# Another order of attention, polar work and weight decoding up to the third unit, and a later last sum of the weights' test

## The chip, the cores and the metric

The kernel runs on one core of a Trainium2 chip. The metric is the device time of one execution in microseconds; a time is the median of several runs. The engines are named as in the profile: PE multiplies matrices, DVE, ACT and POOL work on vectors, SP issues most of the transfers. "The profile" and "the trace" are those of one execution that the hardware profiler recorded.

## What is computed

Three stages follow one another. A linear attention with a complex decay for each channel, a feed-forward layer whose negative half is scaled by alpha, and a layer with eight experts, of which each token takes one:

```python
# attention: B, H, S, D = 4, 8, 768, 48
scale = np.minimum(mag, 0.999) / (mag + 1e-06)
for t in range(S):
    new_re = ar * S_re - ai * S_im
    new_im = ar * S_im + ai * S_re
    S_re, S_im = (new_re + k[t] v[t]^T, new_im)
    y[t] = q[t] @ S_re
# moe: 3072 tokens, 384 -> 2048 -> 384
h = x @ w_in
g = np.maximum(h, 0.0) + alpha * np.minimum(h, 0.0)
x = g @ w_out
# moe2: 8 experts, 384 -> 1024 -> 384
e_idx = np.argmax(x @ w_gate + modality_bias[modality_id], axis=1)
out[e_idx == e] = gate_w * (np.maximum(x @ w1[e], 0.0) @ w2[e])
```

The weights `w_in` and `w_out` of the second stage come as 64-bit floating point numbers.

## The kernel before

**Attention.** The sequence is cut into 6 chunks of 128 tokens, and with 4 batches that makes 24 steps k. For each step, or pair of steps, `polar_group` (L679 on) turns the decays into angles and lengths, runs three scans along the chunk (L737) and writes `z`, which holds the transformed q and k: four multiplications, L774 and L776 twice. `bounce` writes z to DRAM (`zd`) and `bounce_back` reads it turned (`qk`). `attn` then takes, in two halves of four heads, the scores `pa` (L807), the masked `at` (L809, on DVE), the transpose `pk` of k (L815) and its copy `ks`, the output `py` (L825), its split into `xt` and `t` (L831, L832), and the state's increment `pu` (L839, L843).

**The second stage.** A unit is 256 tokens, two steps. `moe1` runs each unit over 8 pairs p of two feature blocks. `l1` makes `ph` (L876, L877, L879; PSUM holds two of them), ACT and DVE make of it `n` (L884, L886), `gh` (L889) and, a turn later, `gl` (L864); `l2` adds to `acc` (L919) two turns later. A unit's first `ph` needs all of its `xt`.

**Decoding.** Each feature block's weights are 64-bit patterns which DVE turns into 32-bit numbers `wf` with three operations (L613, L616, L619), two blocks at a time. `weights_part` then takes a rounded copy on ACT (L566) and the rest on DVE (`w`, L567), and PE transposes the second half (`pl`, L571) so that the routing weights can be multiplied in (`og`, L585).

**The third stage** runs in units named s, t and f with `p2` (L486, L487, L490), `hh`, `hl` (L494), `a2` (L505); its weights `wr` are loaded and split into `wh` and `wl` (L475) as it goes. Beside it a test goes over the weights of the second stage (`ck`, `cm`, L967, L970), whose result `weights_flag` reduces to one number: on DVE (`fw_m`, L977), by a transpose on PE (`fw_t`, L980) and on DVE again (`fw_1`, L982; `fw_i`, L984). Its value enters `more`, which decides on a general fallback, and which SP loads into a register.

**What sets the order.** The program issues instructions to five in-order queues through a scheduler, so an engine takes its instructions in the order that the queue has, and waits where an operand is not there. Up to the third unit the order of issue is spelled out in two strings. START is done before `moe1`, TURN[g] at turn g of it. Each letter is one call: `x`, `y` one DVE operation of the polar work of steps 0 and 1, `q` of steps 2 and 3, `p` of steps 4 and 5; `A`, `a` a part of the attention of steps 0 and 1, `B` of steps 2 and 3, `C` of steps 4 and 5; `D` decodes a pair of weight blocks, `F` finishes one; `b`, `c` issue the bounces of z0 and z1, `d` the rest of the weight loads, `w` the warm-up of 28 products on z1; `<` and `>` switch on and off a link that keeps each step behind the last DVE instruction of the one before. `issue_after(i)` likewise puts what follows behind instruction i.

## Time and profile before

| | us |
|---|---|
| median of 3 runs | 913.98 |
| lowest and highest run | 911.38, 915.74 |
| the profiled execution | 912.0 |
| its span | 910.3 |
| busy: PE, DVE, ACT, POOL | 827.3, 676.0, 467.8, 209.3 |
| mean granted clock of PE | 0.957 of full |

The span is that of the instructions, the execution's own time has 1.7 us around it. "Busy" is the time in which an engine has an instruction running; PE's sum says nothing of the clock at which it runs, which the profile gives separately, as a part of full speed. In the timelines a bracket tells how long the engine was idle ahead of a row and which engine's result ended that.

### The profile page before, as it was taken

Reading aid. Unit: us, or ns where it says so; the run is one execution under the profiler, and the core shown is the slowest. Engines: PE = TensorE matmul, PEld = TensorE weight load, DVE = VectorE, ACT = ScalarE, POOL = GpSimd, SP = SyncE. Lnnn points to the kernel's source line nnn. Section 1 sums busy time; section 2 is a strip of 40 time slices with the busy share of each in tenths; the row PEclk is TensorE's granted clock in tenths of the full one; section 3 lists DMA queues with packets and bytes.
Section 4 is the critical chain, followed back from the end, with each engine's and each line's share of the span. In section 5 each row is a group of like instructions: output and inputs, shape, how many; then the busy total and the mean of one; then the engine's idle time right before and its main releaser. Section 6 shows DMA issues by size and latency. Waiting matters only on the chain.

```text
span 910.3 us, 16047 instructions
## 1 busy us (share of the span) xinstructions
PE 827.3 (91%) x5949; PEld 788.5 (87%) x5949; DVE 676.0 (74%) x1419; ACT 467.8 (51%) x871; POOL 209.3 (23%) x204
## 2 busy tenths in 40 slices
PE   0768978999979999999999999899999999999893
PEld 0658977989979999999999999899988888999893
DVE  7988797999978888878898989455644755666751
ACT  7634446856655655565656564232344445456450
POOL 2001311212102121211212121000332543534550
PEclk9858989999989999999999999999999999999997
DMA  8829400626455326262727261600355477677550
GB/s 330 249 99 317 138 1 4 205 98 176 135 137 154 66 102 152 89 166 67 189 66 189 67 188 32 144 23 6 123 168 143 152 231 258 202 232 268 162 181 20
DMA packets 63591, 130.37 MB, mean 143 GB/s; under 512 B 10456, under 2 KB 39656, under 8 KB 63504
## 3 DMA queue, kind: packets, MB, share of 16 engines
q1 hardware_dynamic: 59536, 119.49, 44.3%
q0 software_dynamic: 3968, 9.77, 3.3%
q8 instruction: 49, 0.80, 0.4%
q14 instruction: 38, 0.31, 0.1%
HBM read 98.17 MB, written 28.91 MB: 140 GB/s over the span
## 4 chain that ended last, share of the span: by engine, by line
PE 52%; DVE 15%; DMA 9%; issue 4%; ACT 1%; POOL 1%; SPq 0%; DVEq 0%; ACTq 0%; POOLq 0%
PE acc L919 12%; PE a2s L505 6%; PE ph L876 5%; PE ph L877 4%; PE ph L879 4%; DMA qk<-zd 4%; DMA zd<-z 3%; PE pa L807 3%; PE p2s L490 2%; DVE n L886 2%; PE p2s L486 2%; PE p2s L487 2%; PE pu L839 2%; PE py L825 1%; PE py L827 1%
## 5 line engine op out<-in xcount | busy, mean ns | idle before, releaser
L876 PE MATMUL ph<-xt,w 128*128 128x256 f32 x576 | 156.0, 299 | 9.6 <-DVE n L886 5.8
L919 PE MATMUL acc<-w,gh 128*128 128x392 f32 x768 | 161.1, 348 | 0.0
L877 PE MATMUL ph<-xt,w 128*128 128x256 f32 x576 | 149.9, 288 | 0.0
L919 PEld LDWEIGHTS acc<-w,gh 128*128 128x128 f32 x768 | 135.1, 192 | 0.6 <-issue 0.5
L876 PEld LDWEIGHTS ph<-xt,w 128*128 128x128 f32 x576 | 112.6, 196 | 11.6 <-DVE n L886 6.2
L886 DVE SCALAR_TENSOR_TENSOR n<-n,al,ph 128x256 f32<-128x256 f32 x192 | 84.1, 473 | 45.2 <-ACT n L884 44.9
L877 PEld LDWEIGHTS ph<-xt,w 128*128 128x128 f32 x576 | 112.9, 196 | 0.2 <-issue 0.2
L879 PE MATMUL ph<-xt,w 128*128 128x256 f32 x576 | 102.5, 287 | 2.1 <-DVE w L567 2.1
L884 ACT ACTIVATE n<-ph 128x512 f32<-128x512 f32 x96 | 57.0, 593 | 78.3 <-PE ph L879 77.3
L919 PE MATMUL acc<-w,gl 128*128 128x392 f32 x384 | 88.7, 345 | 0.0
L889 ACT CAST gh<-n 128x512 fp32r<-128x512 f32 x96 | 59.2, 617 | 57.2 <-DVE n L886 54.8
L864 DVE TENSOR_TENSOR gl<-n,gh 128x512 fp32r<-128x512 f32 x96 | 66.8, 696 | 27.8 <-ACT gh L889 27.7
L879 PEld LDWEIGHTS ph<-xt,w 128*128 128x128 f32 x576 | 84.1, 194 | 2.4 <-DVE w L567 2.3
L268 POOL DMA_INDIRECT tbl<-tok,ix x24 | 27.4, 1141 | 201.7 <-DVE ix L266 191.7
L807 PE MATMUL pa<-qk 96*128 96x128 f32 x384 | 57.0, 296 | 14.9 <-DMA qk<-zd 12.6
L919 PEld LDWEIGHTS acc<-w,gl 128*128 128x128 f32 x384 | 69.8, 190 | 0.4 <-issue 0.3
L807 PEld LDWEIGHTS pa<-qk 96*128 96x128 f32 x384 | 53.4, 207 | 18.0 <-issue 7.7
L494 DVE SCALAR_TENSOR_TENSOR hls<-p2s,hhs 128x512 fp32r<-128x512 f32 x32 | 22.0, 688 | 32.0 <-ACT hhs L493 32.0
L809 DVE TENSOR_TENSOR at<-pa,mask 128x512 f32<-128x512 f32 x48 | 32.9, 684 | 16.2 <-PE pa L807 11.3
L505 PE MATMUL a2s<-whs,hhs 128*128 128x384 f32 x128 | 43.9, 343 | 0.0
L825 PE MATMUL py<-at,v 128*64 128x128 f32 x384 | 43.7, 296 | 0.0
L505 PE MATMUL a2s<-wls,hhs 128*128 128x384 f32 x128 | 43.6, 340 | 0.0
(361 smaller groups left out, 1892.5 us busy)
## 6 DMA issues: line engine op xcount, KB each, us to landing
zd<-z SPq DMA_DIRECT2D x24, 771.0 KB, 4.4
qk<-zd SPq DMA_DIRECT2D x24, 771.0 KB, 7.5
wraw<-in_w_io_dram SPq DMA_DIRECT2D x16, 768.0 KB, 11.9
wrs<-in_wcat_dram SPq DMA_DIRECT2D x32, 384.0 KB, 3.9
ck<-in_w_io_dram SPq DMA_DIRECT2D x16, 768.0 KB, 5.0
wrf<-in_wcat_dram SPq DMA_DIRECT2D x24, 384.0 KB, 4.3
wa<-in_pa__dram SPq DMA_DIRECT2D x10, 768.0 KB, 4.4
wq<-in_pq__dram SPq DMA_DIRECT2D x10, 768.0 KB, 8.9
```

The lines of the kernel that those rows point to most:

```text
L505: nc.tensor.matmul(acc[t], x[:, 128 * t:128 * t + 128], w[:, DM:], start=(f == 0 and x is hh and w is wh), stop=(last and x is hl))
L807: nc.tensor.matmul(pa[:, i, :], kt[:, h, :], qt[:, h, :CH], start=True, stop=True)
L809: self.last = nc.vector.tensor_tensor(at, pa, self.mask.unsqueeze(1).to_broadcast([128, 4, CH]), ALU.mult).ins
L825: nc.tensor.matmul(o, v[:, h * D:h * D + 64], ats[g][:, i, :], start=True, stop=(c == 0))
L864: return engine.tensor_tensor(gl, nf, gh.bitcast(F32), ALU.subtract).ins
L876: nc.tensor.matmul(ph[:, i, :], w1(fc, 0, c), xt[:, c, 0, :], start=(c == 0), stop=False)
L877: nc.tensor.matmul(ph[:, i, :], w1(fc, 0, c), xt[:, c, 1, :], start=False, stop=False)
L879: last = nc.tensor.matmul(ph[:, i, :], w1(fc, 1, c), xt[:, c, 0, :], start=False, stop=(c == 2)).ins
L884: nc.scalar.activation(nf, ph, AF.Relu, scale=-1.0)
L886: paced = nc.vector.scalar_tensor_tensor(nf[:, i, :], nf[:, i, :], self.al1[:, 2 * p + i:2 * p + i + 1], ph[:, i, :], ALU.mult, ALU.add).ins
L889: copy = nc.scalar.copy(gh, nf).ins
L919: nc.tensor.matmul(acc[t][:, :XW], x[:, i, 128 * t:128 * t + 128], self.w[2 * p + i][:, h, DM:], start=(p == i == h == 0 and x is gh), sto ...
```

## The change

START and TURN are rewritten, and the reduction for the weights' flag is split in two. In the core of the diff the two strings are cut to their beginnings, since the rows below say what they do:

```diff
-START = 'xy x2 y2 xy<x y2 x<y>y x2 yx< x2 yxyx y2 > x4 ...
-TURN = ('BF B2', 'B4', 'BLD F2', '', 'D2 F', 'FDFD', ...
+START = 'x2 y x2 y2 x y3 x2 y x2 y3 < x3 y x y x < x3 > x y ...
+TURN = ('B', 'D2 > B F2 B2 D B3', 'B L D F3', '', 'D', 'D F p', ...
...
         m = cp.tile([128, 1], F32, name="fw_m", tag="fw_m", bufs=1)
-        nc.vector.tensor_reduce(m, self.small, axis=AX.X, op=ALU.max)
+        with self.tc.issue_after(self.hl):
+            nc.vector.tensor_reduce(m, self.small, axis=AX.X, op=ALU.max)
+        yield
         pool, tag, bufs = self.bank()
...
-        return fi
+        yield fi
...
     def checked():
-        tabs["fl"] = em.weights_flag(tabs["fl"])
+        tabs["fl"] = next(tabs["w"])
+
+    def flagged():
+        tabs["w"] = em.weights_flag(tabs["fl"])
+        next(tabs["w"])
...
-    at(ng + CK + CW * NFC + 2 * CD, checked)
+    at(ng + CK + CW * NFC + 2 * CD, flagged)
+    at(ng + CK + CW * NFC + 2 * CD + 4, checked)
```

The multiplications, loads and sums are the same in number and size; what differs is where they stand in the queues. From the polar work of steps 6 and 7 on, the queues of both kernels read alike up to the flag.

On DVE, in the polar work of steps 2 and 3 (z_453 is z of step 2, z_470 and z_462 that of step 3; wf_459 and wf_460, or wf_475 and wf_476, the second weight pair), before:

```order
L774 TENSOR_TENSOR z_453<-p_1_128,p_2_129 128x3x128
L613 TENSOR_SCALAR wf_459<-wraw_141 128x768
L613 TENSOR_SCALAR wf_460<-wraw_143 128x768
L616 SCALAR_TENSOR_TENSOR wf_459<-wraw_141,wf_459 128x768
L616 SCALAR_TENSOR_TENSOR wf_460<-wraw_143,wf_460 128x768
L619 SCALAR_TENSOR_TENSOR wf_459<-wraw_141,wf_459 128x768
L619 SCALAR_TENSOR_TENSOR wf_460<-wraw_143,wf_460 128x768
L776 TENSOR_TENSOR z_453<-p_1_128,p_2_129 128x3x128
L774 TENSOR_TENSOR z_470<-p_1_128,p_3_130 128x3x128
L776 TENSOR_TENSOR z_470<-p_1_128,p_3_130 128x3x128
L774 TENSOR_TENSOR z_470<-p_1_128,p_2_129 128x3x128
```

And now:

```order
L774 TENSOR_TENSOR z_453<-p_1_128,p_2_129 128x3x128
L776 TENSOR_TENSOR z_453<-p_1_128,p_2_129 128x3x128
L774 TENSOR_TENSOR z_462<-p_1_128,p_3_130 128x3x128
L776 TENSOR_TENSOR z_462<-p_1_128,p_3_130 128x3x128
L774 TENSOR_TENSOR z_462<-p_1_128,p_2_129 128x3x128
L776 TENSOR_TENSOR z_462<-p_1_128,p_2_129 128x3x128
L613 TENSOR_SCALAR wf_475<-wraw_141 128x768
L613 TENSOR_SCALAR wf_476<-wraw_143 128x768
L616 SCALAR_TENSOR_TENSOR wf_475<-wraw_141,wf_475 128x768
L616 SCALAR_TENSOR_TENSOR wf_476<-wraw_143,wf_476 128x768
L619 SCALAR_TENSOR_TENSOR wf_475<-wraw_141,wf_475 128x768
L619 SCALAR_TENSOR_TENSOR wf_476<-wraw_143,wf_476 128x768
```

The six operations of decoding have passed from the middle of z of step 2 to behind both z.

On DVE, further on, in the attention of steps 2 and 3 (at_0 and at_1 are the two halves of a step; wf_710 and wf_711 are the fourth pair of weights), before:

```order
L886 SCALAR_TENSOR_TENSOR n_0_600<-n_0_600,al_109,ph_0_568 128x256 x2
L613 TENSOR_SCALAR wf_710<-wraw_242 128x768
L886 SCALAR_TENSOR_TENSOR n_1_692<-n_1_692,al_109,ph_1_660 128x256 x2
L864 TENSOR_TENSOR gl_0_698<-n_0_600,gh_0_604 128x512
L809 TENSOR_TENSOR at_0_513<-pa_0_508,mask 128x512
L613 TENSOR_SCALAR wf_711<-wraw_244 128x768
L616 SCALAR_TENSOR_TENSOR wf_710<-wraw_242,wf_710 128x768
L809 TENSOR_TENSOR at_1_543<-pa_1_538,mask 128x512
L616 SCALAR_TENSOR_TENSOR wf_711<-wraw_244,wf_711 128x768
L619 SCALAR_TENSOR_TENSOR wf_710<-wraw_242,wf_710 128x768
L832 TENSOR_TENSOR t_2_561<-py_552,t_2_561 128x128
L809 TENSOR_TENSOR at_0_621<-pa_0_616,mask 128x512
```

And now, from the first mask of step 2 (wf_560 and wf_561 are the fourth pair, w_590 is a lower half of the second, w_598 and w_607 those of the third; the fifth pair follows):

```order
L809 TENSOR_TENSOR at_0_505<-pa_0_500,mask 128x512
L613 TENSOR_SCALAR wf_560<-wraw_242 128x768
L567 TENSOR_TENSOR w_590<-wf_476,w_590 128x768
L616 SCALAR_TENSOR_TENSOR wf_560<-wraw_242,wf_560 128x768
L613 TENSOR_SCALAR wf_561<-wraw_244 128x768
L619 SCALAR_TENSOR_TENSOR wf_560<-wraw_242,wf_560 128x768
L616 SCALAR_TENSOR_TENSOR wf_561<-wraw_244,wf_561 128x768
L809 TENSOR_TENSOR at_1_573<-pa_1_568,mask 128x512
L619 SCALAR_TENSOR_TENSOR wf_561<-wraw_244,wf_561 128x768
L567 TENSOR_TENSOR w_598<-wf_552,w_598 128x768
L567 TENSOR_TENSOR w_607<-wf_553,w_607 128x768
L832 TENSOR_TENSOR t_2_624<-py_615,t_2_624 128x128
```

Decoding and lower halves that stood behind or ahead now stand between the masks; the first mask of step 3 comes nine rows after these, behind the decoding of the fifth pair, and n of pair 1 behind that.

On PE, around the first scores of step 2 (pa_0_508 before, pa_0_500 now; w_431 and w_440, or w_435 and w_444, are the first weight pair), before:

```order
L877 MATMUL ph_2_751<-xt_151,w_718 128x256
L876 MATMUL ph_2_751<-xt_151,w_718 128x256
L877 MATMUL ph_2_751<-xt_151,w_718 128x256
L807 MATMUL pa_0_508<-qk_479 128x128 x4
L815 MATMUL pk_0_515<-ident,qk_479 128x96 x4
L919 MATMUL acc_0_791<-w_431,gh_0_604 128x392 x2
L919 MATMUL acc_1_792<-w_431,gh_0_604 128x392 x2
L807 MATMUL pa_1_538<-qk_479 128x128 x4
L815 MATMUL pk_1_545<-ident,qk_479 128x96 x4
L825 MATMUL py_552<-at_0_513,v_250 64x128 x4
```

And now:

```order
L877 MATMUL ph_1_693<-xt_151,w_582 128x256
L919 MATMUL acc_0_840<-w_435,gh_0_550 128x392 x2
L919 MATMUL acc_1_841<-w_435,gh_0_550 128x392 x2
L919 MATMUL acc_0_840<-w_444,gh_0_550 128x392 x2
L919 MATMUL acc_1_841<-w_444,gh_0_550 128x392 x2
L807 MATMUL pa_0_500<-qk_471 128x128 x4
L815 MATMUL pk_0_507<-ident,qk_471 128x96 x4
L571 MATMUL pl_601<-ident,wf_552 128x128 x3
L571 MATMUL pl_610<-ident,wf_553 128x128 x3
L879 MATMUL ph_1_693<-xt_151,w_582 128x256 x3
L815 MATMUL pk_1_575<-ident,qk_471 128x96 x3
L807 MATMUL pa_1_568<-qk_471 128x128 x4
```

The scores have passed from behind the products of pair 2 to a place in the middle of pair 1 (ph_1), and all of acc's first eight products stand ahead of them.

## Rows read from the trace of the kernel before

**Rows 1.** the page: busy time and share; the clock in 40 slices, in tenths

```profile
PE 827.3 (91%) x5949; PEld 788.5 (87%) x5949; DVE 676.0 (74%) x1419; ACT 467.8 (51%) x871; POOL 209.3 (23%) x204
...
PEclk9858989999989999999999999999999999999997
```

**Rows 2.** windows: stretch, its length, busy time by engine, clock, DMA share, GB/s

```profile
40.20:59.30 19.10, 17.00 (x100) 15.40 (x100) 13.47 (x20) 8.12 (x18) 0.00 (x0) 0.50 0.56 217
59.30:79.60 20.30, 11.76 (x67) 10.39 (x67) 19.95 (x32) 7.78 (x16) 3.39 (x2) 0.67 0.57 156
79.60:100.00 20.40, 20.40 (x163) 18.51 (x163) 13.27 (x22) 7.31 (x18) 0.36 (x2) 0.89 0.90 334
100.00:130.00 30.00, 24.99 (x169) 23.37 (x167) 28.19 (x40) 14.48 (x32) 11.13 (x18) 0.92 0.14 23
130.00:142.10 12.10, 11.60 (x70) 11.29 (x71) 6.74 (x13) 5.63 (x13) 0.36 (x2) 0.78 0.01 2
...
255.00:590.00 335.00, 327.90 (x2687) 320.24 (x2688) 277.03 (x621) 183.71 (x328) 60.03 (x48) 0.99 0.45 121
```

**Rows 3.** PE's timeline: start, length, line, operation, count, [idle before <-releaser]

```profile
27.31 9.14 PE L180 MATMUL warm<-z,ident 128*128 128x128 f32 x56 [27.31 <-DVE z L776]
37.06 1.16 PE L807 MATMUL pa<-qk 96*128 96x128 f32 x8 [0.61 <-DMA qk<-zd]
...
40.19 2.08 PE L807 MATMUL pa<-qk 96*128 96x128 f32 x8 [1.64 <-DVE at L809]
...
67.37 0.87 PE L571 MATMUL pl<-ident,wf 128*128 128x128 f32 x3 [4.62 <-DVE wf L619]
...
79.60 2.08 PE L807 MATMUL pa<-qk 96*128 96x128 f32 x8 [0.47 <-DMA qk<-zd]
...
130.50 0.58 PE L876 MATMUL ph<-xt,w 128*128 128x256 f32 x1 [3.90 <-DVE n L886]
...
177.84 1.16 PE L807 MATMUL pa<-qk 96*128 96x128 f32 x8 [0.66 <-DMA qk<-zd]
```

**Rows 4.** windows and DVE's waits (total, times, longest) of 70.3 to 142 us

```profile
70.30:142.00 71.70, 63.66 (x446) 59.12 (x446) 57.06 (x86) 31.63 (x68) 15.24 (x24) 0.88 0.45 139
...
142.00:177.90 35.90, 31.39 (x212) 30.45 (x210) 33.45 (x50) 27.57 (x51) 6.18 (x7) 0.95 0.34 99
...
DVE n L886 <- ACT n L884: 3.5, 3, 1.7
DVE at L809 <- PE pa L807: 3.5, 3, 2.1
DVE m L687 <- ACT e L684: 2.8, 1, 2.8
DVE xt L832 <- ACT xt L831: 2.0, 1, 2.0
```

**Rows 5.** DVE's timeline, end of steps 0 and 1

```profile
22.95 0.56 DVE L749 SCALAR_TENSOR_TENSOR x<-e,x 128x384 f32<-128x384 f32 x1
23.42 0.95 DVE L737 TENSOR_TENSOR_SCAN s<-first_inverse,s 128x384 f32<-128x384 bf16 x1
```

**Rows 6.** DVE's timeline, around the second weight pair

```profile
63.60 1.02 DVE L613 TENSOR_SCALAR wf<-wraw 128x768 int32<-128x768 int32 x2
...
66.27 1.82 DVE L619 SCALAR_TENSOR_TENSOR wf<-wraw,wf 128x768 int32<-128x768 int32 x2
...
74.76 1.82 DVE L567 TENSOR_TENSOR w<-wf,w 128x768 fp32r<-128x768 f32 x2
```

**Rows 7.** timelines of DVE, PE and ACT at the weights' flag

```profile
846.43 5.18 DVE L970 SCALAR_TENSOR_TENSOR cm<-cm 128x768 f32<-128x768 f32 x1
...
851.87 0.27 PE L980 MATMUL fw_t<-ident,fw_m 128*1 128x128 f32 x1 [1.18 <-DVE fw_m L977]
...
853.48 0.83 ACT L474 CAST whf<-wrf 128x768 fp32r<-128x768 f32 x1 [5.60 <-DMA wrf<-in_wcat_dram]
```

## Prediction

> **What bounds the kernel now.** I read the table of the page first: PE is busy for 827.3 us of the span, and its clock is at 5 tenths in the third of the 40 slices [rows 1]. The windows then say where PE is not busy: in the long middle it works nearly all the time, so nothing is to be had there, while from 100 to 142 us and before 80 us it has holes [rows 2]. The changed order of decoding and attention ends before 178 us (from the fourth polar pair on the rows of all engines stand as they stood, up to the weights' flag at the end), so I went through PE's own timeline to that point. It waits 27.31 us for the last z of step 1, runs the 9.14 us of warm-up, and then loses time to DVE: 1.64 us for a mask result, 4.62 us for the decoding of the second weight pair, later 3.90 us for a correction of n [rows 3]. DVE in turn loses time to PE and ACT between 70.3 and 142 us: of 71.70 us it works 57.06, and the waits that the trace names add up to 14.4 us, in seven groups of which the four largest are shown [rows 4]. So before 142 us neither engine is the bound alone; they wait for each other in turn, and an order that fills DVE's waits with decoding is worth something up to those 14.4 us. From 142 us to the first scores of step 4 at 177.84 us there are 35.9 us in which DVE works 33.45 [rows 4], and in the middle PE is the bound [rows 2]. An advance of both engines at 142 us is therefore handed on to the end.

> **The change part by part.** No instruction on data is added or removed. Every term is the place of an instruction.

> Start, steps 0 and 1. The z of step 0 is finished ahead of the third of step 1's preparations: L749, two scans, and one multiplication (L765) pass behind it, 0.56, 0.95, 0.95 and again some 0.56 us [rows 5], less about 0.09 us of overlap each, so 2.7 us. The first twenty ops of the two steps now take turns, so that some five neighbours no longer read one another; I estimate the overlap that they win by the same 0.09 us at 0.5 us, and z0 comes 3.2 us earlier. The bounce to DRAM of z0 therefore starts earlier, but it is hidden: the warm-up reads z1, starts when z1 is there and lasts 9.14 us, and PE's first scores stand behind it, only 0.61 us late for qk [rows 3]. z1 itself gains only that 0.5 us. So the first scores gain that 0.5 us and at most the 0.61 us, bound 0 to 1.1 us; I take 0.5 us for now. If the cover of the warm-up were gone, the 3.2 us would count.

> Attention of steps 0 and 1, and the first l1. The transposes of k and the sums pu are put between the score products. These 19.1 us hold 17.0 us of PE work at half clock [rows 2], the same work in both orders. I put it at nothing, bounds plus and minus 2 us (the 1.64 us wait, [rows 3], may go or come). The transposes of the second weight pair no longer stand second in ph_0; the 4.62 us wait [rows 3] does not go, it moves behind ph_0, since the decoding that it waits for is itself moved back. What it gives is that n_0 is there for DVE before step 2's scores.

> Steps 2 and 3. The six decode ops of the second weight pair stand between the third and the fourth op of z2, from 63.60 us to the end of the last at 66.27 + 1.82 = 68.1 us, 4.4 us with the overlap taken off [rows 6]. They pass behind all of z2 and z3. Both bounces start 4.4 us earlier, and qk with them; the first scores of step 2, which started at 79.60 us after a 0.47 us wait for qk [rows 3], start at about 75.1 us. DVE does the same work by the end of this decoding, so it gains nothing there by itself (about 70.4 us in both). Of the moved bounce every DMA goes along: SP issues z2, z3, qk2, qk3, then the six last weight loads and the next two polar loads, in the same order as before; only the loads of v of steps 4 and 5 pass behind, and the first reader of those comes after 177 us.

> The stretch from 70.3 to 142 us. This is the term that counts, and it can be seen from either engine. On DVE: its 14.4 us of waits [rows 4]. The 3.5 us for the scores of steps 2 and 3 go, since these are 4.4 us earlier on PE while DVE is where it was, and decoding of three further pairs now stands between them. The wait for xt, part of that for n, and the three groups not shown are 2.0, some 1.4 and 2.6 us, 6 in all; the ops of w8 to w11 that came later in the row now stand in these gaps, and I count 4 of the 6 as filled. At the end of the stretch stand 2.8 us for ACT's square and the rest of n; these follow PE's 3.90 us hole and a stretch at 0.78 of the clock [rows 2, 3], and I count 2 of the some 5 us. That makes 3.5 + 4 + 2 = 9.5 us, bounds 0 and 14.4. On PE: it starts step 2 4.5 us earlier, and of the holes up to 142 us (62.5 us with 20.40 + 24.99 + 11.60 = 57.0 us of work [rows 2]) 5.5 us can go, so at most 10.0 us. I go by the lower of the two limits, 9.5 us; the 0.5 us of the start are inside PE's figure and not added.

> The price of that order. at_0 of step 3 now stands behind the decoding of w8 and w9, and n_1 behind that at; n_2 comes behind the lower halves of w8 to w11. ph has two buffers, so PE can be two pairs ahead of DVE and no more. From the first scores of step 2 to its last py, PE's row now holds 88 matmuls as the trace counts them, two for each product of unrounded numbers: 16 for the scores, 16 for py, 16 for pu, 16 transposes of k, 6 of weights and 18 of ph. In 79.6 to 100 us 163 took 20.40 us at a clock of 0.89 [rows 2], 0.125 us each, so these take 11.0 us, and PE is there at 75.1 + 11.0 = 86.1 us. DVE's rows ahead of t of step 2 after 70.4 us (four each of L613, L616, L619 and L567, by the pairs of [rows 6] 2.0 + 3.6 + 3.6 + 3.6 us, n and two masks some 2 us more, less overlap) end at 84.9 us. So DVE waits 1.2 us there, which is new, and of the 9.5 us I take 8.3.

> The flag at the end. The reduction fw_m goes behind the hl of its turn, and the transpose, the sum and `more` four turns on. Before, PE's fw_t waited 1.18 us for fw_m, which stood behind a sum of the weights' test that took 5.18 us [rows 7]. But the p2f behind fw_t needs a ph buffer that the late hl behind the same sum frees, and the next chain is that of ACT waiting 5.60 us for a DMA of weights [rows 7]. The transpose was therefore covered: gain 0.1 us by the place of fw_m, which stands ahead of that hl, bounds 0 and 1.2 us. Four turns on, two short sums and `more` stand on DVE ahead of its next work, and a register load on SP ahead of a weight load; no row shows their price there, and I bound it by half of the same 1.2 us as a loss. I take a gain of 0.2 us, near the covered case.

> Sum against the profiled execution of 912.0 us: 912.0 - 8.3 - 0.2 = 903.5 us. The median of the runs is 2.0 us above that execution; half of that added gives 904.5 us.

> **The rivals.** *Half clock in the mixed stretch* (same). In 40.2 to 59.3 us PE works 17.0 of 19.1 us and the clock is still 0.50; in 79.6 to 100 us it is 0.89 with a full PE [rows 2]. Busy alone did not bring the clock up in the first, and the new stretch from 75 us has more of the small transposes and waits than the old. If the 88 matmuls up to t of step 2 run at half, they take 11.0 by 0.89 by 2 = 19.6 us and end at 94.7 us; DVE waits 9.8 us at t instead of 1.2, the gain is used up, and the time is 912 us, with 909 and 914 as its ends. For it: the third slice of the page, 45 to 68 us, stands at 5 tenths and the fourth, to 91 us, at 8 [rows 1], so the clock rises only just there. Against: the old stretch from 79.6 us, of the same products, ran mostly at full. [...]

> *Half clock up to 100 us* (slower). The same mechanism, longer: the 20.40 us of PE work at 0.89 [rows 2] are 18.2 us at full and 36.3 us at half. That is 15.9 us lost, less the 8.3 gained: 912.0 + 7.6, with the runs' offset 920.5 us. A microsecond at half instead of 0.89 loses 0.44, so it decides against the change once half clock lasts for 8.3 / 0.44 = 19 us after 75 us. Against it: no stretch with ph products stayed at half so long; ph and acc, the products of the middle with its clock of 0.99 [rows 2], make up most of the work after 85 us.

> *The clock rises earlier than before* (faster still). With fewer holes after 60 us, the 0.67 of that stretch could rise; 11.76 us of work there [rows 2] at full would be shorter by some 4 us, and PE would wait for qk less. 898 us.

> *The order changes nothing* (same). DVE's waits before 142 us are replaced by others of the same size, for instance at t of step 2 and at ACT's square, and qk lands no earlier because the loads of weights still fill the queues: the 4.62 us wait of PE returns and 0 to 2 us are won: 913 us.

> **How the numbers follow.** The forecast, 904.5 us with its own range 899.5 to 909, gets 0.60. The earlier clock gets 0.06, half clock in the mixed stretch 0.18 (with 0.04 of it still faster by over 0.5%), no change 0.09, half clock up to 100 us 0.07. About 0.5%, 4.6 us, is what a measurement of this kernel can tell from no change. Faster: 0.60 + 0.06 + 0.04 = 0.70; same: 0.14 + 0.09 = 0.23; slower 0.07. The range from 897.5 to 913 leaves out the slower rival, half of the no-change case, the upper end of half clock in the mixed stretch and the lower of the earlier clock, some 2 in 10.

> **What would show it.** z2 done some 4 us earlier and the first scores of step 2 near 75 us; DVE's waits from 70 us to the sum of squares of step 4 (L687) near 6 us instead of 14.4; that sum near 133 us instead of 142; the first scores of step 4 near 169 us instead of 177.84, with the clock of 75 to 85 us not below what it was; from there the same distance to the end. Wrong would be a wait of several microseconds of DVE at t or at_0 of step 3, a clock of 0.5 after 80 us, or an advance at 178 us that is gone at 600 us.

## The result

The changed kernel takes 902.6 us (median of 4 runs, 899.5 to 905.3) against 912.7 us (4 runs, 911.2 to 915.7): a ratio of 0.988, with a 95% interval of 0.984 to 0.993. It is faster by 10 us, and its time lies 1.9 us below the forecast of 904.5 us, inside the range. The profiled execution took 901.1 us, with a span of 899.4. The size came out; most of the reason did not, as the runs below show.

The page of the changed kernel, busy time and the clock of PE in 40 slices (of before: [rows 1]):

```profile
PE 822.4 (91%) x5949; PEld 783.4 (87%) x5949; DVE 673.3 (75%) x1419; ACT 466.6 (52%) x871; POOL 204.8 (23%) x204
...
PEclk9978698999999999999999999899999999999997
```

The work is the same. The third slice, which was 5 tenths, is now 7. The windows of the same stretches as [rows 2] (length, busy time of PE, PEld, DVE, ACT and POOL, clock, DMA share, GB/s):

```profile
40.20:59.30 19.10, 13.34 (x113) 11.83 (x114) 19.10 (x30) 8.30 (x20) 0.00 (x0) 0.82 0.56 219
59.30:79.60 20.30, 17.13 (x131) 15.50 (x130) 19.93 (x30) 10.00 (x21) 0.36 (x2) 0.83 1.02 317
79.60:100.00 20.40, 16.83 (x113) 14.11 (x111) 15.72 (x25) 7.39 (x18) 1.78 (x2) 0.83 0.51 176
100.00:130.00 30.00, 28.55 (x181) 27.73 (x182) 24.49 (x39) 14.79 (x33) 8.88 (x18) 0.83 0.06 14
130.00:142.10 12.10, 12.10 (x89) 12.10 (x89) 9.96 (x15) 9.51 (x18) 2.91 (x5) 1.00 0.00 1
...
255.00:590.00 335.00, 328.88 (x2696) 321.52 (x2696) 274.94 (x626) 182.46 (x326) 59.23 (x47) 0.98 0.44 116
```

From 40.2 to 59.3 us the clock is 0.82 where it was 0.50, and DVE, which waited for 5.6 us there, is busy for all 19.1 us. That is the attention of steps 0 and 1, for which the prediction put nothing. PE's timeline shows where it begins (start, length, line, operation, count, idle before and its releaser; of before: [rows 3]):

```profile
27.73 8.45 PE L180 MATMUL warm<-z,ident 128*128 128x128 f32 x56 [27.73 <-DVE z L776]
36.72 1.16 PE L807 MATMUL pa<-qk 96*128 96x128 f32 x8 [0.54 <-DMA qk<-zd]
...
38.95 0.55 PE L815 MATMUL pk<-ident,qk 96*128 96x96 f32 x4 [0.74 <-ACT ks L817]
...
40.13 1.16 PE L807 MATMUL pa<-qk 96*128 96x128 f32 x8 [0.17 <-DVE at L809]
...
52.89 0.87 PE L571 MATMUL pl<-ident,wf 128*128 128x128 f32 x3 [3.50 <-DVE xt L832]
...
63.56 0.90 PE L571 MATMUL pl<-ident,wf 128*128 128x128 f32 x3 [2.71 <-DVE wf L619]
...
69.72 1.06 PE L807 MATMUL pa<-qk 96*128 96x128 f32 x8
...
148.97 0.58 PE L876 MATMUL ph<-xt,w 128*128 128x256 f32 x1 [4.15 <-DVE n L886]
...
169.52 1.16 PE L807 MATMUL pa<-qk 96*128 96x128 f32 x8
```

Before, PE stood idle for 1.64 us ahead of the second scores of step 0, and these took 2.08 us, at half clock. Now transposes of k (38.95) and sums of pu stand in that hole, the idle time is 0.74 and 0.17 us, and the same scores take 1.16 us. The scores of step 2 start at 69.72 us instead of 79.60, those of step 4 at 169.52 instead of 177.84.

The stretch that the forecast rested on lies, in the changed kernel, between the end of the second pair's decoding at 64.3 us and the sum of squares of step 4 at 130 us. Its window, and then DVE's named waits (total, times, longest), five groups (of before: [rows 4]):

```profile
64.30:130.00 65.70, 60.22 (x404) 55.39 (x404) 55.14 (x85) 31.42 (x70) 11.03 (x22) 0.83 0.43 135
```

```profile
DVE gl L864 <- ACT gh L889: 4.4, 2, 3.4
DVE at L809 <- PE pa L807: 2.1, 2, 1.8
DVE t L832 <- ACT t L831: 1.8, 1, 1.8
DVE n L886 <- ACT n L884: 1.1, 2, 0.7
DVE state L843 <- PE pu L839: 1.1, 1, 1.1
```

The stretch lasts 65.7 us instead of about 71.3; the named waits are 10.5 us instead of 14.4. So, in these two profiles, of an advance of 11.7 us at the sum of squares, 6.0 us were there at 64 us already, and 5.7 came in the stretch itself.

### The profile page after: what moved, and what is told of

Read it like the earlier page. It is cut to its first block, busy times and chain, and to the rows that moved or that the text cites. A ratio compares the mean times of both kernels' runs of the same rounds, so it can differ in the third digit from the quotient of the medians.

```text
span 899.4 us, 16054 instructions
## 1 busy us (share of the span) xinstructions
PE 822.4 (91%) x5949; PEld 783.4 (87%) x5949; DVE 673.3 (75%) x1419; ACT 466.6 (52%) x871; POOL 204.8 (23%) x204
## 4 chain that ended last, share of the span: by engine, by line
PE 61%; DVE 16%; DMA 8%; issue 4%; ACT 3%; POOL 1%; SPq 0%; DVEq 0%; ACTq 0%; POOLq 0%
PE acc L919 14%; PE a2s L505 6%; PE ph L876 6%; PE ph L879 5%; PE ph L877 5%; PE pa L807 4%; DMA zd<-z 3%; DMA qk<-zd 3%; PE p2s L490 2%; PE p2s L486 2%; PE p2s L487 2%; DVE n L886 2%; PE py L825 2%; PE pu L839 2%; PE og L585 1%
## 5 line engine op out<-in xcount | busy, mean ns | idle before, releaser
L919 PE MATMUL acc<-w,gh 128*128 128x392 f32 x768 | 159.0, 345 | 0.4 <-ACT gh L889 0.4
L864 DVE TENSOR_TENSOR gl<-n,gh 128x512 fp32r<-128x512 f32 x96 | 66.6, 694 | 33.5 <-ACT gh L889 33.4
L889 ACT CAST gh<-n 128x512 fp32r<-128x512 f32 x96 | 59.3, 617 | 57.2 <-DVE n L886 54.7
L807 PE MATMUL pa<-qk 96*128 96x128 f32 x384 | 54.0, 285 | 10.6 <-DMA qk<-zd 9.8
L807 PEld LDWEIGHTS pa<-qk 96*128 96x128 f32 x384 | 50.5, 197 | 13.3 <-issue 7.5
L474 ACT CAST whs<-wrs 128x768 fp32r<-128x768 f32 x32 | 26.3, 834 | 30.8 <-PE a2s L505 17.0
```

The costliest lines, as they stand in the source:

```text
L807: nc.tensor.matmul(pa[:, i, :], kt[:, h, :], qt[:, h, :CH], start=True, stop=True)
L864: return engine.tensor_tensor(gl, nf, gh.bitcast(F32), ALU.subtract).ins
L889: copy = nc.scalar.copy(gh, nf).ins
L919: nc.tensor.matmul(acc[t][:, :XW], x[:, i, 128 * t:128 * t + 128], self.w[2 * p + i][:, h, DM:], start=(p == i == h == 0 and x is gh), sto ...
```

## The experiments

Each batch was timed beside runs of the kernel before on the same chip: medians 915.7 us (17 runs) for the first four, 914.8 us (18) for the next four, 913.1 us (11) for the last four. The profiled execution of before, 912.0 us, was thus one of the faster ones, and leads are better read between runs than against it alone.

### The parts of the change

**Flag alone**: before with only `weights_flag` split.

```diff
+        with self.tc.issue_after(self.hl):
+            nc.vector.tensor_reduce(m, self.small, axis=AX.X, op=ALU.max)
+        yield
```

> Only the split of the weights' flag; both order strings as before. Theory A (the trace of the changed kernel): the split is worth 2.2 us, since before it the idsf and wrf loads on SP stood behind the register load of more, and PE fell to half clock there. Then the lead stays at 0 us up to 850 us and is 2 to 2.5 us at the end, the time near 910.5 us. Theory B (the prediction): the transpose was covered, 0.2 us, 912.5 us, and the 2.2 us of the changed kernel came from another phase of its third stage.

915.4 us, ratio 1.001 (0.998 to 1.004): nothing that can be measured. Theory A's 2.2 us would be a ratio of 0.998, at the very edge of the interval; what speaks against it more clearly is PE's wait for DVE near the end of the third stage, in the run with the split alone and then in the one with the old flag and the new strings:

```profile
860.91 0.90 PE L379 MATMUL ptf<-ident,xgf 128*128 128x128 f32 x3 [2.65 <-DVE hlf L494]
```

```profile
847.15 0.89 PE L379 MATMUL ptf<-ident,xgf 128*128 128x128 f32 x3 [0.92 <-DVE hlf L494]
```

The wait is long with the split and short without it, so it was not the split that made it 1.04 us in the changed kernel, where before had 2.17. What did is not shown.

**Both strings** (START and TURN as changed, flag as before), **START alone** (with a last `D`, which the old TURN needs), and **TURN alone**:

```diff
+START = 'x2 y x2 y2 ... q7 F q5 D d D'     # START alone
```

> Only the two order strings; the flag as before. Theory A: 8.4 us less than before up to 850 us and the same at the end, the time near 904.5 us. Theory B: 10.6 us less at the end, near 902.5 us. The clock of PE at 40 to 59 us, 0.82 in the changed kernel and 0.50 before, is near 0.8 again if it comes from the order, and may be 0.5 if it changes from one execution to the next.

> Only the first string (with one decoding at its end, that the second string of before needs); the second string and the flag as before. Theory A: the gain up to 64 us (6 us, from the attention of steps 0 and 1 at full clock) belongs to this string, so step 2's scores come some 8 us earlier and about 6 us are left at the end unless the old order of the second string takes them back: 906.5 us. Theory B (the prediction's sum): steps 0 and 1 give nothing, only z2 and z3 come 4.4 us earlier; DVE's waits of unit 1 stay, 2 to 4 us are left: 909 us.

> Only the second string (the first without its last decoding); the flag as before. Theory A: it has no part in the 6 us up to 64 us and gives 2 to 4 us in the stretch of 70 to 142 us: 909.5 us. Theory B (the prediction's sum): it gives the larger part, 6 of 8.3 us, by filling DVE's waits: 906 us. PE's clock at 40 to 59 us is 0.5 by A, as before.

902.8 us (0.985, 0.981 to 0.988), 904.7 us (0.989, 0.984 to 0.993) and 906.1 us (0.990, 0.986 to 0.993). The strings are the whole gain. But each alone seems to give 10 to 11 us and both 13. START alone has two pairs of runs, 899.2 and 901.0 us with a mean clock of 0.971, and 908.4 and 908.5 us with 0.963 to 0.964, so its median describes neither; the profile is that of 899.2 us. And TURN alone was not expected to reach the attention of steps 0 and 1, where its queues are those of before. Its clock there, in windows of 4 us (length, PE busy, clock, DMA share, GB/s):

```profile
36.00:40.00 4.00, 1.53 (x13) 1.00 1.12 249
40.00:44.00 4.00, 4.00 (x25) 0.57 1.00 410
44.00:48.00 4.00, 4.00 (x44) 1.00 1.01 414
```

It fell at 40 us as before, after a hole of 1.36 us, but came back at 44 us, whereas in the profiles of before and of the flag alone it stayed at half to about 70 us, although PE's row is the same there. So what follows that hole differs between executions, and a comparison of the strings needs the clock held equal.

### The clock, with the order kept

**Dummy work in the hole**: the kernel before, and five products behind the first transposes of k.

```diff
+FILL = {(0, 0): 5}
...
+                if (k, g) in FILL:
+                    with self.tc.issue_after(tr):
+                        self.fill(FILL[k, g])     # products of the identity with itself
```

> The kernel before, with five products of the identity added behind the first transposes of k of step 0, whose result nobody reads, so that PE works in the 1.64 us in which it waited for the first mask. No other instruction moves. Theory C (clock): that hole is what lets PE's clock fall to half from 40 us on; with it filled the clock stays at full up to the wait at 57 us, the second weight pair is decoded 5 to 6 us earlier and about 4 to 6 us are left at the end: 909 to 911 us against 915. Theory D (work): the changed kernel gains there because transposes and pu are done in the hole, 1.2 us of work; dummy work brings nothing and the time stays at 915 us.

907.3 us, ratio 0.990 (0.986 to 0.994). Work that nobody needs makes the kernel 7.5 us faster, so theory D cannot be all of it. The six runs lie in two groups, 903.0 to 904.6 us with a mean clock of 0.967, and 910.0 to 911.5 us with 0.962 to 0.964. The profile is one of the upper group, and shows a second hole, ahead of the first scores (PE's timeline, then windows):

```profile
38.08 2.08 PE L815 MATMUL pa<-qk 96*128 96x128 f32 x8 [2.18 <-DMA qk<-zd]
```

```profile
36.00:40.00 4.00, 1.92 (x9) 0.75 1.14 228
40.00:44.00 4.00, 4.00 (x21) 0.50 1.00 381
44.00:48.00 4.00, 4.00 (x41) 0.90 1.01 414
```

The warm-up had ended 2.18 us before qk landed, and the clock fell there. (The dummy work itself shows as x10, two records for each product.) It does not always: in TURN alone a wait of 2.21 us at the same place left the clock at 1.00.

**The hole put back**: the changed kernel, with the second transposes of k and pu of step 0 held behind the second scores.

```diff
+                with self.tc.issue_after(sc) if k == 0 and g == 1 else nullcontext():
                     ... pk transposes
+              with self.tc.issue_after(sc) if k == 0 else nullcontext():
                 ... pu
```

> The changed kernel, with the second transposes of k and pu of step 0 held behind the second scores, so that PE's order in the attention of steps 0 and 1 is that of before and its hole is back; the rest as changed. Theory C: the clock falls to half at 40 us again, in most executions for the whole attention, the second weight pair is decoded 4 to 6 us later, and the time is 906 to 908 us instead of 902.6. Theory D: only the 1 to 2 us of moved work are lost: 904 us. By the prediction's sum, which gave this place nothing, 902.6 us.

910.6 us, ratio 0.994 (0.991 to 0.997), slower than any of the three forecasts. PE's second scores, and the clock that follows (windows as above):

```profile
40.25 2.08 PE L807 MATMUL pa<-qk 96*128 96x128 f32 x8 [1.82 <-DVE at L809]
```

```profile
40.00:52.00 12.00, 11.75 (x64) 0.50 0.81 321
```

With the hole the clock is at half again, z of step 3 is done at 67.2 us instead of 60.0, and 6 to 8 us of the change's gain are gone. Taken out by dummy work or put back by an order, the hole acts in both directions. And what is left with the hole in both kernels, 4.2 us against before, is a first measure of the rest of the order.

### The prediction's main step, by itself

**z of steps 2 and 3 ahead of the second pair's decoding**, without and with the dummy work:

```diff
-... q7 > q4 D q18 Fqr q3 D q3 d>D'
+... q7 > q4 D q18 Fqr q6 D d>D'
```

> The kernel before, with one edit in its first string: the second weight pair is decoded after z of steps 2 and 3 instead of between them. The prediction's step: z2 and z3 and the first scores of step 2 come 4.4 us earlier, DVE's 3.5 us of waits for these scores go, and 3 to 4 us are left: 911.5 us against 915. Theory E: PE has then nothing to do until the decoding comes, and the later attention meets it at half clock; at most 1 us is left: 914 us.

> Both of these edits in the kernel before: the five dummy products and z of steps 2 and 3 ahead of the second pair's decoding. If the two act on different waits, their gains add: by theory C and the prediction's step 7 to 9 us, 906 to 908 us; if both gain the same slack, no more than the larger of the two: 909.5 us.

914.4 us, ratio 0.999 (0.996 to 1.002), and 905.2 us, 0.989 (0.986 to 0.992). The step brings the scores forward and nothing that can be measured in the time (PE's first scores of step 2, DVE's sum of squares of step 4):

```profile
76.30 2.05 PE L807 MATMUL pa<-qk 96*128 96x128 f32 x8
```

```profile
142.39 0.96 DVE L687 TENSOR_TENSOR m<-m,e 128x768 f32<-128x768 f32 x1 [2.77 <-ACT e L684]
```

The scores start 3.4 us earlier than in the run of the flag alone (79.67), and the sum of squares stands where it stood there (142.37); both profiles are of executions among the longer of their kernels, 919.8 and 918.1 us. In this profile PE's clock was at half from 41 to 82 us; that the earlier scores ran slowly, and so gave their lead back, fits this but was not tested. With the dummy work the scores come at 69.24 us and the sum at 132.6 us, 6.1 and 2.8 us ahead of the run with both holes closed below. Of that the times show nothing clear: 905.2 us is 2.1 us less than the dummy work alone, with runs from 901.3 to 909.1.

### The order, with the clock kept

**Both holes closed** in before: the dummy work, and 34 instead of 28 products in the warm-up. **The longer warm-up in the changed kernel. TURN alone with both.** And the changed kernel with the longer warm-up and **twelve dummy products in its 3.50 us wait** at 49 us.

```diff
-WN = 28
+WN = 34
...
+FILL = {1: 12}     # the last of the four: behind the first pl
```

> The kernel before with the five dummy products, and 34 instead of 28 products in the warm-up, so that it lasts until qk of step 0 has landed. Theory C: with both holes closed (2.18 us ahead of the first scores in the profile of the run with the five products alone, and 1.64 us ahead of the second) no execution falls to half clock before the wait at 49 us; all runs lie in the faster of that kernel's two groups (903 to 905 us), none in the slower (910 to 911.5 us): median 903.5 us. If the groups have another cause, both appear again and the median stays near 907 us.

> The changed kernel with 34 instead of 28 products in the warm-up. Theory C: its wait of 0.54 us for qk goes, the rest stays: 901 to 903 us with less spread than 899.5 to 905.3. The difference from the kernel before with both holes closed is then what all of the change's order is worth at equal clock: by the prediction's sum 8 us, by theory C no more than 1 to 3 us.

> Only the second string changed, with the dummy products and the longer warm-up. It tells whether the second string is worth anything at equal clock: by theory C it lies within 2 us of the kernel before with both holes closed, 902 to 904 us; if the second string gives 4 us or more by itself, 899 to 900 us.

> The changed kernel with the longer warm-up and twelve dummy products (3.5 us at full clock) behind the first transposes of weights, where PE waits 3.50 us and its clock falls to half from 52 to 70 us. If PE's clock matters there, the first scores of step 2 come 1 to 2 us earlier and the time is 900 to 901 us. If DVE is the bound there (it has no wait named from 42 to 70 us), nothing moves: 902 us.

905.5 us (0.993, 0.990 to 0.995), 901.4 us (0.987, 0.984 to 0.989), 902.5 us (0.988, 0.985 to 0.991) and 903.6 us (0.990, 0.988 to 0.992). The first has its holes closed (PE's dummy work, the window):

```profile
39.25 1.31 PE L188 MATMUL fill<-ident 128*128 128x128 f32 x10
```

```profile
40.00:52.00 12.00, 9.81 (x105) 1.00 0.88 344
```

Its runs spread from 902.6 to 909.3 us, not as one narrow group, so that part of theory C missed. What sets them apart is not shown: only the run of 902.8 us was profiled. Between the first and the second what differs, beside the five dummy products and the flag, is the order of the change, at equal clock up to 52 us: 4.0 us, with spreads of 902.6 to 909.3 and 898.2 to 902.3 that do not meet, and close to the 4.2 us with the hole in both. TURN alone seems to have 3.0 of them, 1 us more than theory C allowed, but its runs, 898.3 to 904.7 us, overlap with the first's. The dummy work at 49 us brought nothing: its six runs, 902.8 to 904.9 us, all lie above those of the second kernel, by 2.2 us in the median; why is not shown. It does not test what the clock is worth there, since the clock of 52 to 70 us was 0.72 with and without it: PE waited 2.32 us for xt later on. That PE's speed is not what that stretch waits for rests on the profile: in the changed kernel DVE was at work from 40.2 to 70 us without a break. The second kernel, 898.2 to 902.3 us, has the lowest median of all, but not clearly better than the changed one with 28 products.

All profiles side by side. The times of events are from their timelines, the clock is that of 40 to 52 us, and L693 is the next operation of the polar work on DVE behind that sum; one execution can be several microseconds off the median beside it:

| kernel | clock | scores step 2 | L687 step 4 | L693 to scores, step 4 | profiled us | median us |
|---|---|---|---|---|---|---|
| before | 0.50 | 79.6 | 141.7 | 33.5 | 912.0 | 913 to 916 |
| flag alone | 0.52 | 79.7 | 142.4 | 35.0 | 918.1 | 915.4 |
| z first | 0.55 | 76.3 | 142.4 | 34.5 | 919.8 | 914.4 |
| changed, hole put back | 0.50 | 77.2 | 136.2 | 36.2 | 910.9 | 910.6 |
| before, dummy work | 0.80 | 77.2 | 137.3 | 36.6 | 911.5 | 907.3 |
| TURN alone | 0.86 | 75.5 | 132.1 | 36.4 | 906.4 | 906.1 |
| before, both holes closed | 1.00 | 75.3 | 135.4 | 34.5 | 902.8 | 905.5 |
| z first, dummy work | 0.96 | 69.2 | 132.6 | 33.1 | 901.3 | 905.2 |
| START alone | 1.00 | 68.3 | 131.8 | 33.1 | 899.2 | 904.7 |
| changed, twelve dummy products | 1.00 | 69.7 | 128.8 | 37.2 | 903.1 | 903.6 |
| both strings | 1.00 | 69.6 | 128.7 | 35.4 | 903.8 | 902.8 |
| changed | 1.00 | 69.7 | 130.0 | 36.7 | 901.1 | 902.6 |
| TURN alone, both closed | 1.00 | 75.0 | 130.4 | 38.3 | 903.0 | 902.5 |
| changed, longer warm-up | 1.00 | 69.9 | 128.5 | 37.6 | 901.5 | 901.4 |

## Why the prediction held in size and not in its reasons

**The attention of steps 0 and 1.** "I put it at nothing, bounds plus and minus 2 us" is the step that failed. I took the 17.0 us at half clock as given for both orders, since the work was the same, and did not ask what the 1.64 us hole in front of them did to the clock. Dummy work in that hole brings 7.5 us, the hole put back costs 6 to 8. A rival with an earlier clock was there at 0.06, but for the stretch after 60 us, and not for the place where it came.

**Steps 2 and 3.** Of the 4.4 us by which the bounce was to come earlier, 3.4 us were left at the scores in the run with that edit alone. The worth of it was mis-sized: 3.5 us of waits in the sum, alone no more than the noise (between 4 us gained and 1.5 lost). In the changed kernel the scores came at 69.72 us instead of the 75.1 forecast. The attention ahead of them adds to the bounce: the clock kept, in the old order, gives 75.3 us, z first 76.3, and both together 69.2.

**The stretch up to 142 us.** Mis-sized: 5.7 us in the profile instead of 8.3, and 4.0 us in the times at equal clock. DVE's wait for t of step 2, 1.2 us by the sum, did not come, since PE, at full clock (1.00 from 69.7 to 78.8 us), ran the new row in 9.1 us instead of 11.0. At step 3 two waits came in its place, 1.8 us for scores that took 1.92 us at half clock (0.50 from 86.6 to 88.5 us) and 1.8 us for t; so the waits for scores went only from 3.5 to 2.1 us instead of to nothing. And a new one of 3.4 us for gh came, behind PE's own products at half clock (0.51 from 100 to 108 us).

**"Handed on to the end."** Wrong by 3.1 us in the two profiles. At L693 of step 4 the profile leads by 11.45 us, at the scores of step 4 by 8.3. By the table the seven kernels with the new TURN need 35.4 to 38.3 us there, the seven with the old one 33.1 to 35.0 us and once 36.6, so the loss is 2 to 3 us and not the same in each. In the old order PE waits twice, 1.99 us for ACT and then 1.86 us for n, behind which it runs at full clock (1.00 from 159 to 166 us); in the changed kernel it waits once, 4.15 us for n (148.97, above), and then runs mostly at half, 0.59 over the next 7 us. Then ACT waits for PE, and DVE for ACT (PE's second wait before; then, of the changed kernel, the timelines of ACT and DVE):

```profile
159.17 0.39 PE L876 MATMUL ph<-xt,w 128*128 128x256 f32 x1 [1.86 <-DVE n L886]
```

```profile
155.93 0.17 ACT L587 COPY of<-og 128x16 f32<-128x16 f32 x1 [3.04 <-PE og L585]
```

```profile
157.77 0.69 DVE L864 TENSOR_TENSOR gl<-n,gh 128x512 fp32r<-128x512 f32 x1 [2.91 <-ACT gh L889]
```

Before, DVE waited 0.33 us at this place. With both strings alone PE waits the same 4.15 us, but its clock is 0.77 over the next 7 us, DVE waits 1.77 us, and the stretch takes 35.4 us.

**The start and the flag.** z of step 0 came 2.7 us earlier and z of step 1 0.05 us, so the 0.5 us estimated for overlap did not come; the first scores came 0.34 us earlier. That z of step 0 is hidden held. The flag is worth nothing measurable, as said.

**The rivals.** Half clock in the mixed stretch did not come where it was put, since the products up to t of step 2 ran at 1.00. It came behind them, at step 3: the windows from 79.6 to 130 us have 0.83 where they had 0.89 and 0.92. The waits of 1.8 and 3.4 us above lie there, but it did not decide. Busy alone did not keep the clock up: in the stretch of before it was 0.50 with PE busy for 17.0 of 19.1 us, and in the same order with dummy work in the holes it was 1.00 from 40 to 52 us. Nor did the number of transposes of k decide it: before and the changed kernel have the same ones there, and from 40 to 52 us one ran at 0.50 and the other at 1.00.

Together: of the 11.7 us by which the changed kernel with the longer warm-up leads before, some 7.6 come from the clock and 4.0 from the order, where 0 and 8.3 had been forecast. That the forecast time came out is thus in part luck: a gain that was put at nothing made up for a stretch, and a handing on, that gave less. What stays open is what decides, after the hole, between half clock for 4 us (TURN alone) and for 30 us (before, flag alone); and where the order's 4 us lie, since no run took TURN apart.

## What to carry to other kernels

Where PE runs at half clock, price the hole ahead of the stretch first, even if it is as short as the 1.64 us here: fill it with useful work, or with work that nobody needs to see what it is worth (7.5 us here), before any order behind it is judged. A lead on one engine's row is worth only what is left at the next place where both engines meet; read it there and again one stage later (here 11.45 us at L693 of step 4 and 8.3 at its scores). And an order should be compared with the clock held equal, since each string alone seemed to bring nearly the whole gain (10 to 11 us of 13).

## What the runs showed of the hardware

Second, one DVE operation of 128x768, the last L970, took 5.17 us in the changed kernel (5.18 before, [rows 7]) while POOL ran two subtractions of the same size; of the others of its kind in the changed kernel one took 2.36 us (750.04), also beside such a subtraction, and the rest 0.94 to 0.95. Two of these, at 786.41 and 816.88 us, overlapped a subtraction on POOL too; there POOL's took 2.28 and 2.44 us instead of 1.84. And the long time does not belong to that one operation: in the run with twelve dummy products another of that size, an L483, took 5.05 us at about the same time, and the last sum 0.94. From the timelines of DVE and POOL in the changed kernel, and of DVE in that run:

```profile
838.01 5.17 DVE L970 SCALAR_TENSOR_TENSOR cm<-cm 128x768 f32<-128x768 f32 x1
```

```profile
838.71 3.65 POOL L475 TENSOR_TENSOR wlf<-wrf,whf 128x768 fp32r<-128x768 f32 x2
```

```profile
837.70 5.05 DVE L483 TENSOR_TENSOR wlf<-wrf,whf 128x768 fp32r<-128x768 f32 x1 [1.08 <-ACT whf L482]
```

POOL's two took 3.65 us, about twice the 1.84 us that one took at 849.11 us, so it was DVE that lost the time at this place. That POOL's work held it up is what the overlap suggests; it was not tested apart, and what POOL ran beside the 5.05 us is not shown.
